# Attention, routed experts and a dense layer in one kernel: early routing moved up, three quarter buffers, and dense rows transposed elsewhere

## The chip, the cores and the metric

One core of a Trainium2 chip. Its engines are PE (matrix multiply), DVE (vector), ACT (activation), POOL (GpSimd) and SP, which here issues most of the DMA. The metric is the device time of one execution in microseconds (us), as a median of runs.

## What is computed

```python
q, k, v: (4, 12, 448, 64) float32
attn = sigmoid(q @ k.T / 8 - log(448)) @ v          # per batch and head
x = attn.transpose(0, 2, 1, 3).reshape(1792, 768)   # tokens
logits = x @ w_gate                                 # 8 experts
e = argmax(logits); g = softmax(logits)[e]          # top 1
x[t] = g[t] * relu(x[t] @ w1[e[t]]) @ w2[e[t]]      # w1 768x1024, w2 1024x768
out = relu(x @ w_in) ** 2 @ w_out                   # 768x2048, 2048x768
```

## The kernel before

All matmuls of the experts and of the dense layer are made three times on a high and a low half of each operand: `split_w` (L461) lets ACT copy the float32 chunk into the high half (L462) and DVE, or POOL where asked, subtract it for the low half (L463). The instructions of each engine run in the order in which the program writes them (a manual schedule), so an engine that waits holds back all that is written behind it. SP's DMA issues are such a queue too.

**Attention** runs over 24 units, one for each batch and pair of heads (loop from L477, n = 0 to 23, `last_n` = 23). In unit n, PE computes the scores of n in four parts, ACT the sigmoids, and PE the products with v of unit n-1 (`av_step`). `rows` (L408) transposes the result of unit n-2 and sends it to x_d in DRAM through ACT (L413, two buffers). After the last pair of a batch `logits` (L383) adds up the gate logits into the tile lgT, of which there is one buffer, and `token_logits` (L400) turns them into one row per token. Beside this, `convert` rewrites the dense weights chunk by chunk: nine of 16 (PRE = 9) in units 2 to 19, the last of them on DVE to the end of unit 19. The other seven follow in steps taken by `rest` (L597).

**Early routing.** After batch 2, `head` (L186) finds each token's expert from the first 12 of 16 groups of rows and adds up the counts (`cum`), `counts` (L200) sums them on PE into p1, which uses lgT's buffer, `early_expert` (L219) picks the fullest expert, `spots` (L211) and `pick_rows` (L215) find its first 256 tokens, and `early_rest` (L234) copies the result from p1. Slots 0 and 1 work on these tokens, so their weights can be loaded (`regs`, `reload`, L304 to L311) and their rows gathered (`early_gather`) while attention still runs. The full routing of all tokens (`head`, `counts`, `slots` L244, `late_places` L260, `spots`, `pick_rows`, `late_rows`) takes place during slot 0 in the function `opening` (L855), and its rest (`late_routing` L790, `quarters` L815, `gates` L827) during slot 2.

**Slots.** NBASE = 15 slots of 128 tokens of one expert each (loop from L884). A slot has eight steps: `up(0)` to `up(3)` multiply by w1, `down(4)` to `down(7)` by w2, each with one weight chunk of 128 x 1536. Between them `htrans` (L679) transposes the hidden rows on PE, ACT writes the high half hh (L683) and DVE the low half hl (L684), for each half of the hidden layer (hl 0 and hl 1 in the prediction). After each step `next_chunk` splits the next slot's chunk, which lies in `raw[c]`, and reloads `raw[c]` for the slot after that, if its expert differs. Chunk 7 is split on POOL (`POOL_W`). At step 5 `xtrans` (L291) transposes the next slot's rows through the two px tiles. In slot 0, `take` splits chunks 4 to 7. From slot 3 on, four *quarters* of 32 leftover tokens are worked off between the steps (`q_event` L743): each has its own eight weight chunks, read from QB = 2 buffers `qraw` by `q_load` (L732), and each load is issued when the buffer before it has been used.

**Into the dense layer.** The slots write their result to y_d. In the last slot (s = 14) the weight ring for the dense layer is filled (`stage`, `load_next`), `rest` takes eight steps, and `trans_y` (L605) transposes the first four row tiles of y_d: one behind the up half, three behind steps 4 to 6. Its two halves lie in weight tiles wh2, wh3, wl2, wl3 (`alloc_y`, L615). Then comes a block `If` (L934) for slots beyond 15, not taken here, and the quarters' writes to y_d on POOL (L954), one after the other. In the dense stage, block 0 has 1024 rows in two halves h: `layer1` (L995) runs 16 times, with four places for `rest` in each (two chunks of conversion take 16). The second half of t_d may be loaded only when all 16 chunks are done (L564).

## Time and profile before

| | us |
|---|---|
| median of 3 runs | 1017.72 |
| lowest, highest | 1012.18, 1018.63 |
| the profiled execution | 1016.02 |
| its span, first to last instruction | 1014.5 |
| PE busy in it | 954.3 |

The profile is of one execution. Its times count from the start of the span. Attention ends on PE at 172.47, slot 0 starts at 185.49, slot 1 at 215.49, slot 2 at 233.92, slot 3 at 261.13, the last slot at 514.93, and the dense stage at 549.95. In the rows, `<-` behind an operation names what was read, and `[4.65 <-POOL Bg L811]` is idle time ahead of it and what ended it. PEld is the loading of PE's weights, and a `q` behind an engine's name its instruction queue. The clock is given as a share of 2.4 GHz.

### The profile page before, as it was taken

Reading aid. Unit: us, or ns where it says so; the run is one execution under the profiler, and the core shown is the slowest. Engines: PE = TensorE matmul, PEld = TensorE weight load, DVE = VectorE, ACT = ScalarE, POOL = GpSimd, SP = SyncE. Lnnn points to the kernel's source line nnn. Section 1 sums busy time; section 2 is a strip of 40 time slices with the busy share of each in tenths; the row PEclk is TensorE's granted clock in tenths of the full one; section 3 lists DMA queues with packets and bytes.
Section 4 is the critical chain, followed back from the end, with each engine's and each line's share of the span. In section 5 each row is a group of like instructions: output and inputs, shape, how many; then the busy total and the mean of one; then the engine's idle time right before and its main releaser. Section 6 shows DMA issues by size and latency. Waiting matters only on the chain.

```text
span 1014.5 us, 15007 instructions
## 1 busy us (share of the span) xinstructions
PE 954.3 (94%) x5869; PEld 799.5 (79%) x5869; DVE 632.4 (62%) x692; ACT 551.2 (54%) x667; POOL 132.1 (13%) x120
## 2 busy tenths in 40 slices
PE   7999999788999999989987799999999999999996
PEld 3555554677887887878876688889999999999996
DVE  3777776668776666775766367626776632227863
ACT  5676665545776676775743354435544434446540
POOL 1000000214422222222220000000000110000002
PEclk9999999888999999998997899999999999999998
DMA  8788868271377769694457446442333442222412
GB/s 291 264 303 326 317 205 287 110 279 51 130 264 273 287 246 338 212 357 145 142 221 271 169 155 230 175 187 68 94 104 130 173 165 68 67 67 94 125 32 93
DMA packets 52512, 190.62 MB, mean 188 GB/s; under 512 B 8083, under 2 KB 18963, under 8 KB 50387
## 3 DMA queue, kind: packets, MB, share of 16 engines
q1 hardware_dynamic: 34290, 152.77, 43.1%
q0 software_dynamic: 6928, 31.08, 8.0%
q10 hardware_dynamic: 11216, 5.75, 2.0%
q8 instruction: 48, 0.79, 0.3%
q14 instruction: 30, 0.24, 0.1%
HBM read 203.33 MB, written 36.98 MB: 237 GB/s over the span
## 4 chain that ended last, share of the span: by engine, by line
PE 75%; DMA 10%; issue 8%; DVE 3%; ACT 2%; POOL 1%; SPq 0%; POOLq 0%; another core or an unknown queue 0%; ACTq 0%; DVEq 0%
PE pq L1103 7%; PE pq L1104 7%; PE pq L1105 7%; PE pp L1003 6%; PE pp L1004 6%; PE pp L1005 6%; PE po L373 5%; PE sc L363 5%; DMA qraw<-in_wm 4%; PE ph L654 3%; PE py L654 3%; PE py L656 3%; PE ph L655 3%; PE py L655 3%; PE ph L656 3%
## 5 line engine op out<-in xcount | busy, mean ns | idle before, releaser
L463 DVE TENSOR_TENSOR wl<-raw,wh 128x1536 fp32r<-128x1536 f32 x98 | 193.1, 1974 | 83.9 <-ACT wh L462 74.6
L462 ACT ACTIVATE wh<-raw 128x1536 fp32r<-128x1536 f32 x112 | 165.9, 1482 | 4.2 <-PE ph L656 2.0
L367 ACT ACTIVATE a<-sc,bias_s 128x896 f32<-128x896 f32 x96 | 82.5, 910 | 55.3 <-PE sc L363 55.1
L1009 ACT ACTIVATE r<-pp 128x512 f32<-128x512 f32 (+1 forms) x64 | 34.8, 544 | 117.0 <-PE pp L1005 117.0
L654 PE MATMUL py<-wh,hh 128*128 128x384 f32 x240 | 88.2, 368 | 3.9 <-ACT hh L683 3.9
L1103 PE MATMUL pq<-wrh,sh 128*128 128x384 f32 x264 | 89.0, 337 | 0.3 <-DVE raw L1064 0.3
L1104 PE MATMUL pq<-wrl,sh 128*128 128x384 f32 x264 | 88.6, 336 | 0.0
L1105 PE MATMUL pq<-wrh,sl 128*128 128x384 f32 x264 | 88.6, 336 | 0.0
L656 PE MATMUL py<-wh,hl 128*128 128x384 f32 x240 | 84.1, 350 | 3.9 <-DVE hl L684 3.9
L655 PE MATMUL py<-wl,hh 128*128 128x384 f32 x240 | 83.7, 349 | 1.3 <-DVE wl L463 1.3
L654 PE MATMUL ph<-wh,xh 128*128 128x512 f32 x180 | 76.9, 427 | 0.0
L463 DVE TENSOR_TENSOR wrl<-raw,wrh 128x1536 fp32r<-128x1536 f32 x30 | 52.7, 1757 | 36.0 <-ACT wrh L462 36.0
L655 PE MATMUL ph<-wl,xh 128*128 128x512 f32 x180 | 72.7, 404 | 0.0
L656 PE MATMUL ph<-wh,xl 128*128 128x512 f32 x180 | 72.7, 404 | 0.0
L462 ACT ACTIVATE wrh<-raw 128x1536 fp32r<-128x1536 f32 x30 | 44.5, 1483 | 47.8 <-PE pq L1105 43.1
L463 POOL TENSOR_TENSOR wl<-raw,wh 128x1536 fp32r<-128x1536 f32 x14 | 49.0, 3500 | 164.6 <-ACT wh L462 164.6
L1030 DVE TENSOR_TENSOR sl<-h,sh 128x1024 fp32r<-128x1024 f32 (+1 forms) x56 | 59.8, 1086 | 8.7 <-ACT sh L1029 8.6
L1017 DVE TENSOR_TENSOR h<-h,h 128x512 f32<-128x512 f32 (+1 forms) x16 | 10.0, 625 | 88.5 <-ACT h L1012 88.5
L373 PE MATMUL po<-a,qkv 128*64 128x448 f32 x288 | 59.4, 548 | 0.0
L1029 ACT ACTIVATE sh<-h 128x1024 fp32r<-128x1024 f32 (+1 forms) x56 | 51.5, 943 | 13.6 <-PE pq L1104 8.0
L978 POOL DMA_INDIRECT out<-raw,idx x14 | 13.7, 978 | 330.8 <-DVE raw L1064 302.3
L1003 PE MATMUL pp<-why,wrh 128*128 128x512 f32 (+1 forms) x132 | 49.2, 373 | 7.5 <-issue 7.5
(274 smaller groups left out, 2200.9 us busy)
## 6 DMA issues: line engine op xcount, KB each, us to landing
raw<-in_wm SPq DMA_DIRECT2D x112, 768.0 KB
qraw<-in_wm SPq DMA_DIRECT2D x32, 768.0 KB
raw<-t_d SPq DMA_DIRECT2D x28, 768.0 KB
cs<-in_w SPq DMA_DIRECT2D x9, 1536.0 KB
raw<-w_d SPq DMA_DIRECT2D x16, 768.0 KB
qkv<-in_qk SPq DMA_DIRECT2D x23, 480.0 KB
raw<-in_w SPq DMA_DIRECT2D x7, 1536.0 KB
t_d<-raw POOLq DMA_DIRECT2D x7, 1536.0 KB, 7.6
```

The costliest lines, as they stand in the source:

```text
L367: nc.scalar.activation(a[:, :n], ps[:, :n, :S], AF.Sigmoid, bias=bias_s, scale=1.0 / math.sqrt(D))
L373: nc.tensor.matmul(po[64 * h:64 * h + 64, :S], vr[:, 128 * c + 64 * h:128 * c + 64 * h + 64], a[:, h], start=(c == 0), stop=False, skip_gr ...
L462: nc.scalar.activation(h, src, AF.Copy)
L463: (nc.gpsimd if pool else nc.vector).tensor_tensor(l, src, f32(h), op=ALU.subtract)
L654: nc.tensor.matmul(ps, lh, rh, start=first, stop=False)
L655: nc.tensor.matmul(ps, lh, rl, start=False, stop=False)
L656: nc.tensor.matmul(ps, ll, rh, start=False, stop=last)
L1003: nc.tensor.matmul(pp[:, :N], lh, rh, start=(k == 0), stop=False)
L1004: nc.tensor.matmul(pp[:, :N], lh, rl, start=False, stop=False)
L1103: nc.tensor.matmul(po[p][:, :DH], lh, wc[:, w0:w0 + DH], start=(q == 0 and kk == 0 and o in (0, 2, 5)), stop=False, **fl)
L1104: nc.tensor.matmul(po[p][:, :DH], lh, wcl[:, w0:w0 + DH], start=False, stop=False, **fl)
L1105: nc.tensor.matmul(po[p][:, :DH], ll, wc[:, w0:w0 + DH], start=False, stop=(q == 3 and kk == 1), **fl)
```

## The change

There are five parts. (1) Early routing: `token_logits` and `head` run at the end of unit 19, `counts`, `early_expert` and `spots` in unit 20, `pick_rows` in unit 21, `early_rest` and both early gathers at the start of unit 22; each of them was a unit later (the gathers stood behind the last unit in the program, though POOL issued them at once). Chunks 0 and 1 of the early expert are loaded in unit 21 into a tile `first` that later is a weight tile, the others go into raw[0] to raw[5]; chunks 0 to 2 are split at the ends of units 21 to 23. (2) Behind the last unit slot 0's rows are transposed between its products, ahead of both row copies; then come the full `head` and the split of chunk 3. (3) In `opening`, counts and slots move to step 0, POOL no longer splits a chunk, spots stays at step 5, and `pick_rows`, `late_rows` and two gathers move to slot 1; `late_routing` moves from slot 2, step 0, to slot 1, step 6, `quarters` to slot 2, step 0, and `gates` with the first quarter loads to step 5. (4) QB is 3; the tile Bg lies in one of the three buffers until gates has read it. (5) In the last slot the four `trans_y` stand behind steps 0 to 3, their two halves lie in the raw buffers of chunks 4 to 7, no `rest` runs there, conversion uses two weight tiles instead of raw buffers, and the loads of the next two row tiles are issued at step 4.

```diff
@@ -43,7 +43,7 @@
-QB = 2
+QB = 3
@@ -162,7 +162,7 @@
-    gp, Bg = rt([CP, NR, 3], "gp", BF16), rt([CP, NR, 3, LC], "Bg", BF16)
+    gp = rt([CP, NR, 3], "gp", BF16)
@@ -303,14 +303,24 @@
-        if s:
+        if s > FS:
...
+    def chunk0(c):
+        return raw[c - 2] if c > 1 else first[:, c * CH:(c + 1) * CH]
...
     def reload(s, c):
-        more_ = dict(cond=regd[s], cond_hint=False) if s else {}
-        nc.sync.dma_start(out=raw[c], in_=wm[ds(rege[s], 1), :, c].rearrange("a p n -> (a p) n"), **more_)
...
+        more_ = dict(cond=regd[s], cond_hint=False) if s > FS else {}
+        dst = raw[c] if s else chunk0(c)
+        nc.sync.dma_start(out=dst, in_=wm[ds(rege[s], 1), :, c].rearrange("a p n -> (a p) n"), **more_)
...
+    def rtile(k, name, dt=F32):
+        return rawp.tile([128, 2 * CH], dt, tag=f"raw{k}", name=name)
...
+    def wpair(w, dt, name):
+        return w1p.tile([128, 2 * CH], dt, tag=f"{w}p", name=name)
@@ -462,6 +472,13 @@
+        def split_first(c):
+            split_w(chunk0(c), wh[c], wl[c])
+            if c == 1:
+                for w, l in (("wh", wh), ("wl", wl)):
+                    both = wpair(w, F32R, f"{w}23")
+                    l.extend([both[:, :CH], both[:, CH:]])
@@ -472,20 +489,25 @@
             if n >= len(units) - 4:
-                rawb.append(rawp.tile([128, 2 * CH], F32, tag="raw", name=f"raw{n}", bufs=4))
+                rawb.append(rtile(n % 4, f"raw{n}"))
...
-                wh, wl = ([w1p.tile([128, CH], F32R, tag=f"{w}{c}", name=f"{w}{c}") for c in range(4)] for w in ("wh", "wl"))
+                wh, wl = ([w1p.tile([128, CH], F32R, tag=f"{w}{c}", name=f"{w}{c}") for c in range(2)] for w in ("wh", "wl"))
+                first = wpair("wl", F32, "first")
+            if n == last_n - 2:
+                regs(0)
+                reload(0, 0)
+                reload(0, 1)
             if n == last_n - 1:
-                regs(0)
-                for c in range(4):
-                    reload(0, c)
+                reload(0, 2)
+                reload(0, 3)
+                early_rest(pr1)
+                xg = {s: early_gather(s) for s in range(FS)}
...
-                early_rest(pr1)
@@ -493,10 +515,7 @@
-            if n == last_n:
-                logits(b, GJ - 1)
-                split_w(raw[0], wh[0], wl[0])
-            elif done and n < last_n - 1:
+            if done:
@@ -504,43 +523,43 @@
-            if due:
+            if due or n == last_n - 4:
                 token_logits()
-            if n == last_n - 2:
+            if n == last_n - 3:
...
+            if n == last_n - 2:
+                pick_rows(pr1, Bt1, FR)
...
+            if n == last_n - 4:
+                head(0, FR)
             if n == last_n - 3:
-                head(0, FR)
-            if n == last_n - 2:
...
-            if n == last_n - 1:
-                pick_rows(pr1, Bt1, FR)
-            if n == last_n:
-                split_w(raw[1], wh[1], wl[1])
+            if n > last_n - 3:
+                split_first(n - last_n + 2)
...
-        extras()
-        for c in range(4):
-            av_step(c)
+        av_step(0)
+        av_step(1)
+        xs = {}
+        tx = [ps_s.tile([128, 2, 512], F32, tag="sc", name=f"tx{i}")[:, 0].rearrange("p (b c) -> p b c", b=4) for i in range(2)]
+        xs[0] = xtrans(0, xg.pop(0), tx)
+        av_step(2)
+        av_step(3)
...
         reload(0, 7)
+        extras()
...
-        xg = {s: early_gather(s) for s in range(FS)}
-        xs = {}
-        tx = ps_s.tile([128, 2, 512], F32, tag="sc", name="tx").rearrange("p a (b c) -> p a b c", b=4)
-        xs[0] = xtrans(0, xg.pop(0), [tx[:, 0], tx[:, 1]])
         token_logits()
-        split_w(raw[2], wh[2], wl[2])
+        head(FR, NR)
+        split_first(3)
...
-        head(FR, NR)
-        split_w(raw[3], wh[3], wl[3])
@@ -580,9 +600,9 @@
         if step < 7:
-            narrow(n, step, rawb[2], rawb[3], None)
+            narrow(n, step, *cv, None)
         if step == 4 and n < 15:
-            narrow(n + 1, 0, rawb[2], None, None)
+            narrow(n + 1, 0, cv[0], None, None)
@@ -596,8 +616,8 @@
         if pool is None:
-            n = 3
-            t = [[wtile(f"{w}{c}", f"{w}y_{bi}_{c}") for c in (2, 3)] for w in ("wh", "wl")]
+            n = 6
+            t = [[x] for x in ([rtile(k, f"yt{k}", F32R) for k in (2, 3)] if bi == 0 else [wpair(w, F32R, f"{w}y_{bi}") for w in ("wh", "wl")])]
@@ -608,17 +628,18 @@
-        per = 3 if n == 3 else 4
+        per = 3 if n == 6 else 4
...
-            for j in js[::n]:
-                dst = yh[j // n][:, :, t * 128:(t + 1) * 128]
-                src = pt[:, j - js[0]:j - js[0] + n]
+            w = min(n, per)
+            for j in js[::w]:
+                dst, low = (x[j // n][:, j % n:j % n + w, t * 128:(t + 1) * 128] for x in (yh, yl))
+                src = pt[:, j - js[0]:j - js[0] + w]
...
-                nc.vector.tensor_tensor(yl[j // n][:, :, t * 128:(t + 1) * 128], src, f32(dst), op=ALU.subtract)
+                nc.vector.tensor_tensor(low, src, f32(dst), op=ALU.subtract)
@@ -807,6 +826,8 @@
+            Bg = mp.tile([128, 2 * CH], BF16, tag="qraw", name="Bg", bufs=QB)[:CP, :NR * 3 * LC].rearrange("p (t a s) -> p t a s", t=NR, a=3)
+            qt["Bg"] = Bg
@@ -824,9 +845,9 @@
         def gates():
-            pg = ps_x.tile([128, 4, 128], F32, tag="px1", name="pgt").rearrange("p a b -> p (a b)")
+            pg = ps_q.tile([128, 512], F32, tag="q", name="pgt")
             for t in range(NR):
-                nc.tensor.matmul(pg[:, :3 * LC], A[:, t, :], Bg[:, t].rearrange("p a s -> p (a s)"), start=(t == 0), stop=(t == NR - 1))
+                nc.tensor.matmul(pg[:, :3 * LC], A[:, t, :], qt["Bg"][:, t].rearrange("p a s -> p (a s)"), start=(t == 0), stop=(t == NR - 1))
@@ -842,32 +863,29 @@
-        def take(c, pool=False):
-            split_w(raw[c], mh[c], ml[c], pool=pool)
+        def take(c):
+            split_w(chunk0(c), mh[c], ml[c])
...
             if c == 0:
-                early_gates()
-                take(4)
-            elif c == 1:
...
-            elif c == 2:
-                take(5)
...
-                take(7, pool=True)
-            elif c == 3:
-                take(6)
-                late_places(prk2)
-                for k in range(8):
-                    reload(FS, k)
+                reload(FS, 0)
+                reload(FS, 1)
+                reload(FS, 6)
+                reload(FS, 7)
+                take(4)
+                early_gates()
+            elif c < 4:
+                take(4 + c)
+                if c == 3:
+                    for k in range(2, 6):
+                        reload(FS, k)
+                    late_places(prk2)
...
-            elif c == 7:
-                pick_rows(pr2, Bt, NR)
-                late_rows(pr2)
-                xg[FS] = gather(FS)
@@ -875,38 +893,38 @@
-            if 0 < s and s + 2 < NBASE:
-                if s > 1:
-                    regs(s + 2)
+            if 1 < s and s + 2 < NBASE:
+                regs(s + 2)
...
+            if last:
+                ynext = alloc_y(0)
...
+                if s == 1 and c == 0:
+                    pick_rows(pr2, Bt, NR)
+                    late_rows(pr2)
+                    for k in range(FS, FS + 2):
+                        xg[k] = gather(k)
...
                     if c == 0:
-                        late_routing()
-                    elif c == 1:
...
                     elif c == 3:
-                        gates()
-                        nc.gpsimd.dma_start(out=yq_d[:, :, DM:DM + 1].rearrange("q t a -> t q a"), in_=tok[:QM, NSLOT:].bitcast(F32).unsqueeze(2))
-                        for n in range(QB):
-                            q_load(n)
...
                 if last:
-                    rest()
+                    trans_y(0, 0, c, ycur[0][c], ynext, ps_x, ("px0", "px1"))
             if last:
-                ynext = alloc_y(0)
-                trans_y(0, 0, 0, ycur[0][0], ynext, ps_x, ("px0", "px1"))
+                cv.extend(wpair(w, F32, f"{w}c") for w in ("wh", "wl"))
+                narrow(PRE, 0, cv[0], None, None)
@@ -914,21 +932,25 @@
+                if s == FS and c == 5:
+                    gates()
+                    nc.gpsimd.dma_start(out=yq_d[:, :, DM:DM + 1].rearrange("q t a -> t q a"), in_=tok[:QM, NSLOT:].bitcast(F32).unsqueeze(2))
+                    for n in range(QB):
+                        q_load(n)
...
+                if s == 1 and c == 6:
+                    late_routing()
...
-                if last and c < 7:
-                    trans_y(0, 0, c - 3, ycur[0][c - 3], ynext, (ps_x, ps_h)[c % 2 == 0], ("px0", "px1") if c % 2 else ("ph0", "ph1"))
+                if last:
+                    if c == 4:
+                        yns = {t: load_y(0, 1, t, xgp, 2, "xg") for t in range(2)}
...
-                if last:
-                    rest()
-            if last:
-                yns = {t: load_y(0, 1, t, xgp, 2, "xg") for t in range(2)}
@@ -1049,7 +1071,9 @@
-        obs = [[rawb[2 + h][:, p * DM:(p + 1) * DM] for p in range(P)] for h in range(2)]
+        if bi == 0:
+            ob = [rtile(k, f"ob{k}") for k in (2, 3)]
+        obs = [[ob[h][:, p * DM:(p + 1) * DM] for p in range(P)] for h in range(2)]
```

## Rows read from the trace of the kernel before

**Rows 1.** The page, part 1: busy us of each engine, share of the span, instructions.
```profile
PE 954.3 (94%) x5869; PEld 799.5 (79%) x5869; DVE 632.4 (62%) x692; ACT 551.2 (54%) x667; POOL 132.1 (13%) x120
```

**Rows 2.** Waits of PE over the span: who, for whom, us in total, times, longest.
```profile
PE pp L1003 <- issue: 7.5, 1, 7.5
...
PE qa L761 <- DMA qraw<-in_wm: 7.5, 3, 3.6
...
PE pyt L616 <- DMA yn<-y_d: 6.9, 1, 6.9
...
PE pgt L829 <- POOL Bg L811: 4.7, 1, 4.7
...
PE py L654 <- ACT hh L683: 3.9, 1, 3.9
```

**Rows 3.** Windows: stretch, length, busy PE, PEld, DVE, ACT, POOL, clock, DMA share, GB/s.
```profile
172.47:185.49 13.02, 8.51 (x42) 4.46 (x43) 4.75 (x6) 4.47 (x7) 0.00 (x0) 0.90 0.94 344
185.49:215.49 30.00, 23.86 (x119) 20.55 (x119) 23.79 (x60) 13.08 (x17) 7.06 (x6) 0.82 0.29 106
215.49:233.92 18.43, 18.43 (x104) 16.71 (x101) 12.86 (x12) 13.86 (x15) 3.66 (x3) 1.00 0.61 236
233.92:261.13 27.21, 22.28 (x116) 19.72 (x116) 22.18 (x40) 15.63 (x18) 13.66 (x12) 0.87 0.26 91
261.13:514.93 253.80, 242.68 (x2008) 207.28 (x2007) 177.97 (x121) 175.35 (x193) 69.39 (x35) 0.97 0.68 245
514.93:542.40 27.47, 23.56 (x117) 20.91 (x116) 16.97 (x21) 12.47 (x19) 5.28 (x2) 0.88 0.52 177
549.95:585.50 35.55, 28.69 (x117) 23.57 (x117) 16.71 (x27) 10.51 (x22) 3.00 (x5) 0.83 0.52 178
```

**Rows 4.** The same view, three stretches right behind a long wait of PE.
```profile
457.60:462.80 5.20, 5.19 (x33) 3.98 (x34) 0.00 (x0) 0.00 (x0) 1.17 (x2) 0.50 0.90 318
528.48:534.47 5.99, 5.99 (x21) 5.67 (x22) 5.26 (x7) 1.96 (x5) 0.00 (x0) 0.50 0.17 33
577.00:582.30 5.30, 5.29 (x19) 4.72 (x20) 2.90 (x9) 1.98 (x6) 0.00 (x0) 0.50 0.00 2
```

**Rows 5.** DVE in order of time, units 19 to 22: start, us, line, operation.
```profile
147.61 0.56 DVE L130 TENSOR_TENSOR cd<-cd 128x384 f32<-128x384 f32 x1
...
151.67 0.24 DVE L191 TENSOR_REDUCE m<-lg 112x12 f32<-112x96 f32 x1
...
153.65 0.44 DVE L197 TENSOR_TENSOR_SCAN cum<-seg,ohz 112x136 bf16<-112x136 bf16 x1
...
161.21 2.08 DVE L213 TENSOR_SCALAR A<-iot,plf 112x128 f16<-112x128 f16 x12
```

**Rows 6.** Chain that ended last, end of attention: start, us, what.
```profile
149.15 0.70 PE lgT L405 x8
...
172.56 8.63 DMA x_d<-xn
```

**Rows 7.** Slot 0, in order of time: POOL, then DVE.
```profile
199.94 3.49 POOL L463 TENSOR_TENSOR wl<-raw,wh 128x1536 fp32r<-128x1536 f32 x1 [3.63 <-ACT wh L462]
...
200.01 3.46 DVE L257 CAST ctl<-esl 128x20 int32<-128x20 f32 x1
```

**Rows 8.** Quarter loads: SP in order of time, then the chain that ended last.
```profile
292.03 0.34 SPq L739 DMA_DIRECT2D qraw<-in_wm  x1
...
300.25 8.97 DMA qraw<-in_wm
```

**Rows 9.** POOL in order of time: the last slot, then two t_d writes.
```profile
517.16 3.50 POOL L463 TENSOR_TENSOR wl<-raw,wh 128x1536 fp32r<-128x1536 f32 x1 [13.82 <-ACT wh L462]
...
592.18 0.90 POOL L131 DMA_DIRECT2D t_d<-raw  x1 [23.20 <-DVE raw L130]
...
663.25 0.89 POOL L131 DMA_DIRECT2D t_d<-raw  x1 [15.59 <-DVE raw L130]
```

**Rows 10.** Line 934 (the If): duration min/median/max in ns, first and last start.
```profile
L934 PEldq COMPARE_BRANCH  x1: 5262/5262/5262, 539.5 to 539.5; - x1
```

More of the change, by code (lines that the diff above doesn't have):

```diff
@@ L334, in load @@
         def load(b, j):
-            rv = rawp.tile([128, 2 * CH], F32, tag="raw", name=f"qkv_{b}_{j}", bufs=4)
+            rv = rtile((b * NP + j) % 4, f"qkv_{b}_{j}")
             r = rv[:, :QW]
```

3 lines of the change are left out of this document (1 added, 2 removed).

## Prediction

> **What bounds the kernel now.** I read the page first, then PE's waits, then windows cut at the borders of the stages, and only then single engines. The page says that PE is busy 954.3 of 1014.5 us [rows 1]: nothing else can be the bound on the whole, and the change can win only the 60 us in which PE stands, plus what it loses at half clock. The list of waits names where [rows 2]: 7.5 us at the first dense matmul, 7.5 us in the first layer of the quarters (weights not landed), 6.9 us for rows of y_d, 4.7 us for the gate products, 3.9 us in the last slot behind ACT. The windows show the same by stage [rows 3]. Slot 1 is the clean one: 18.43 us, PE never idle, clock 1.00; that is the price of a slot without quarters. Slot 0 takes 30.00, slot 2 27.21, the last slot 27.47, and 13.02 lie between the last unit's end and slot 0. After a long wait PE runs on at a granted clock of 0.50, the 1.2 GHz level [rows 4]; there each us yields half. So a wait costs itself and some 2.5 to 3 us behind it.
>
> **The change part by part.** The sum is made against the profiled execution, 1016.02 us (span 1014.5 and 1.5 around it), which lies 1.7 below the median 1017.72. A plus is time lost.
>
> *Early routing a unit sooner (units 19 to 22), +3.9.* PE is never idle here, so each new wait is a loss. DVE ends the w_out conversion at 148.17 (147.61 + 0.56), and head takes 2.42 (151.67 to 154.09) [rows 5]. Now token_logits comes a unit earlier (0.70 on PE [rows 6], moved, not added), and head runs straight behind the conversion: cum is ready at 148.2 + 0.7 + 2.4 = 151.3. PE asks for it with counts where its scores end, 149.15 + 0.70 = 149.85 [rows 6]: 1.4 of wait. Behind head, and a unit on behind spots (2.08 of DVE [rows 5]), the split of the next q and k comes late by about 0.5 in all (estimate from the same durations). Third, logits now opens a new lgT tile in unit 22, which frees only when early_rest has copied pr1; on DVE early_rest stands behind the first weight split, which waits for ACT, which waits for the last sigmoid and for chunk 0. I follow the queues to 2.0 of wait. If chunk 0 needed the 9.0 from issue to landing that a weight load needs under load [rows 8] and not the some 4 that I assume, it would be 7. Bounds of this part: +1 and +8. Queued behind the waiting split on ACT are the sigmoids, for which PE waits in turn. SP has no other work there (all q, k, v loads are out), POOL's two gathers move up with nothing behind them.
>
> *Between the last unit and slot 0, -5.1.* PE is busy 8.51 of 13.02, part of it at the low clock [rows 3]. In the chain the 8.63 us of an x_d write end the wait [rows 6]: ACT stands before the row copy, and the transposed x of slot 0 stands behind it. Now that x is transposed before both row copies, its gather is out somewhat earlier, and chunks 0 to 2 are split. I count 6.3 of PE work and 1.6 of waits (logits on the last xT, DVE being behind split 2): 7.9. Bounds -7 and -2.
>
> *Slot 0, -7.2.* DVE is busy 23.79 of 30.00 [rows 3]. One CAST of 20 columns took 3.46 us because POOL's split of chunk 7 (3.49) ran beside it [rows 7]; one of the twelve small operations of spots takes 0.17 [rows 5]. The change gives that split to DVE and drops chunk 2's, so DVE keeps about 20.5 us, more than PE's 18.43. The queue order (slots and two splits ahead of hl 0, late_places ahead of hl 1) adds some 2.3: 22.8. Bounds 18.9 (PE alone) and 27. Slot 2's eight weight loads lose their condition; they ran before too (slots 0 and 1 moved 30.00 us at 106 GB/s and 18.43 at 236 [rows 3], 7.5 MB, of which 6.3 are such weights). The Trainium skill's page "SBUF — State Buffer", section "SBUF: two separate sides", says that GpSimd and VectorE share one port pair, that whoever starts first holds it for the whole instruction, and that the other stands still. By that rule the 3.46 goes wholly, as the row says, but it comes back in slot 2, below.
>
> *Slots 1 and 2, +0.4 and -2.3.* pick_rows (some 0.4) moves into slot 1. late_routing moves from slot 2 to the end of slot 1, quarters to slot 2's start, gates to its second half. The wait for the gate products (4.7 [rows 2]) goes, but what is late next is hl 0: ahead of it DVE has the same work, late_routing, two splits and quarters, in all 22.18 busy in 27.21 [rows 3]; only the idle time of DVE at slot 1's end (18.43 against 12.86 busy) is won. I take a wait of 3.5 and 1.5 of low clock on 18.43 + 0.5 (gates) + 1.0 (order on PE): 24.9. Bounds: 22 and 27.4. If POOL's products and its split of chunk 7 each stop DVE wholly, as the quoted rule has it, 3.5 comes on top and the part wins nothing.
>
> *Three quarter buffers, -15.0.* Slots 3 to 13: 253.80, PE busy 242.68, so 11.1 idle, nearly all of it for quarter weights, and a clock of 0.97, up to 7.6 lost, of which I count 5 (one such stretch is 5.20 at 0.50 [rows 4]). The worst kind of load was issued at 300.25 and landed 8.97 later, too late by a wait of the order of 2 to 3.6 [rows 2, 8]. With three buffers each load is issued at the place of the one before, here 292.03 [rows 8], 8 us sooner: more than any wait. The number of loads is the same. Bounds -16.5 and 0.
>
> *Last slot, -5.5.* Without the conversion steps ACT no longer stands before the copy of hh: 3.9 of wait and half of 5.99 [rows 2, 4] go, 6.9. The four tiles' transposes are the same number of instructions, now in the up half. Their low parts go where chunk 7 lies, which POOL reads until 520.66 [rows 9], 5.7 us into the slot; DVE waits, the second tile's transposes wait for their px tile: 1.4 back. Bounds -7 and -3.
>
> *Into the dense stage, -1.0 and -8.5.* PE stands 7.5 at line 934. Its branch alone took 5.26 [rows 10], and the DMA rings were full with a 1.5 MB t_d write, which now comes later; I take 1.0 (0 to 4). The Trainium skill's "Runtime: NRT & Kernel Launch", section "Instruction fetch mechanics", says that a taken branch has to wait for its code by DMA; by it the gap stays and the sum is 1.0 less. The wait for rows of y_d (6.9, then half of 5.30 [rows 2, 4]) goes: POOL no longer stands at the If for the t_d write, its four quarter writes start some 9 sooner, and two of the loads are issued in the last slot. I take 8.5 of 9.5; bounds 0 and 9.5.
>
> *Rest of the dense stage, +0.7.* Eight conversion steps move here, 56 into 64 places. Their DVE time is hidden behind PE. The last t_d write comes two calls later: its cover is gone by some 16 us, see below. 0 to +4.
>
> Sum: +3.9 - 5.1 - 7.2 + 0.4 - 2.3 - 15.0 - 5.5 - 1.0 - 8.5 + 0.7 = -39.6. 1016.0 - 39.6 = 976.4 for a profiled execution, 978 with the 1.7 of the median.
>
> **The rivals.**
> 1. *Quarter loads stay late.* When a slot's weights are reloaded too, the DMA engines run at a share of 0.90 and more (first row of [rows 4]); an earlier issue would only queue longer. For it: the low stretches lie there. Against: the mean share of slots 3 to 13 is 0.68 [rows 3]. Time: 978 + 15 = 993.
> 2. *The early part gives it back.* Chunk 0 lands late and ACT stands before the sigmoids (+4.1), slot 0 is 27 (+4.2), POOL stops DVE in slot 2 (+2.3): 978 + 10.6, about 989. For it: DVE is the fuller engine in slots 0 and 2. Against: the splits 0 to 2 are out of the way. The Trainium skill's page "SBUF — State Buffer" stands on its side for the third term.
> 3. *The dense rows are late all the same*, as the quarters' writes to y_d still end last: the 9.5 stay, 978 + 9.5, about 988.
> 4. *Slower: conversion ends last.* All seven chunks are now converted inside dense layer 1 of block 0, and the loads of the second half of t_d wait for the last write. A chunk is eight steps, two calls of sixteen; the last is done in call 14, and write and load leave some 5 us of margin. Four cycles took 71.07 together, 17.8 each [rows 9], where 17.1 would be the pace. It decides from 17.1 + (39.6 + 5) / 7 = 23.5 a cycle; at 26 it costs 7 x 8.9 - 5 = 57, which gives 1035. Against: a cycle would have to grow by half.
>
> **How the numbers follow.** Forecast 0.55, its own range 968 to 987. Rival 1 0.13, rival 2 0.15, rival 3 0.06, rival 4 0.05; several of the first three with other losses, ending within 1% of before, 0.06. About 1% (10 us) is what a measurement of this kernel can tell from no change. Faster by more: 0.55 + 0.13 + 0.15 + 0.06 = 0.89; within: 0.06; slower: 0.05. The range of 8 in 10 takes the forecast and rivals 1 to 3 without their worst ends, and on the low side parts with better bounds (-4 in slot 0, -3 at the If, -2 between): 964 to 999.
>
> **What would show it.** Right: waits on qraw gone and slots 3 to 13 near 237 to 239; slot 0 near 23; last slot near 22, with a wait of DVE on POOL's split in its first third; no wait on yn; no CAST over 1 us in slot 0; new waits of PE on cum in unit 20 and on the copies of pr1 in unit 22. Wrong: PE standing on hl in slot 2 as long as before, loads of qraw landing over 12 us after issue, a wait of the first pq on the split of ring chunk 9, or attention longer by over 8 us.

## The result, and the profile after

The changed kernel takes 982.77 us (median of four, 979.62 to 985.92) against 1017.5 for the kernel before (four runs, 1012.18 to 1018.63): a ratio of 0.967, 95% interval 0.962 to 0.972. The forecast was 978, its range 964 to 999. The profiled execution took 985.92 us with a span of 984.1, which is 30.4 less than before, where 39.6 had been worked out.

First the waits of PE over the whole span of the changed kernel (who, for whom, us in total, times, longest).

```profile
PE py L677 <- DVE hl L703: 8.4, 4, 6.0
PE sc L373 <- DMA qkv<-in_qk: 5.9, 1, 5.9
PE pyt L636 <- DMA yn<-y_d: 5.8, 1, 5.8
PE lgT L401 <- DVE sa L237: 4.9, 1, 4.9
PE pp L1027 <- issue: 4.4, 1, 4.4
PE p L201 <- DVE cum L197: 1.4, 1, 1.4
PE pyt L636 <- DVE yt L642: 1.3, 1, 1.3
```

Against [rows 2]: the waits on qraw, on Bg and on hh are gone. The 5.9 at sc is the first load of the kernel, which no part of the change touches. New are sa (the copies of pr1, in unit 22), cum and yt. The waits on yn and at the branch are smaller, but they stayed. The wait on hl has moved and grown: 6.0 of it now lie in slot 2, where the kernel before had its longest, 3.3, in slot 0 (at 209.01) and 0.3 in slot 2:

```profile
PE py L656 <- DVE hl L684: 3.9, 3, 3.3
```

Next the windows, cut at the stages as in [rows 3] (length, busy us of PE, PEld, DVE, ACT, POOL, granted clock, DMA share, GB/s): end of attention to slot 0, slots 0, 1 and 2, slots 3 to 13, the last slot; then three stretches at half clock, each of which begins while PE still waits (until 166.43, 244.77 and 546.69); then the dense stage from PE's return after the branch.

```profile
180.98:188.76 7.78, 7.65 (x43) 3.59 (x43) 4.47 (x6) 3.69 (x6) 0.00 (x0) 1.00 0.82 265
188.76:210.58 21.82, 19.43 (x103) 16.54 (x103) 20.34 (x60) 12.36 (x15) 3.56 (x5) 1.00 0.62 234
210.58:229.48 18.90, 18.90 (x115) 16.98 (x115) 12.87 (x12) 14.08 (x16) 3.71 (x3) 1.00 0.39 140
229.48:256.39 26.91, 20.95 (x115) 18.83 (x115) 23.61 (x40) 15.63 (x18) 12.60 (x11) 0.87 0.16 50
256.39:493.91 237.52, 237.15 (x2008) 203.19 (x2007) 177.94 (x121) 175.34 (x193) 68.10 (x37) 1.00 0.73 267
493.91:516.07 22.16, 20.81 (x117) 18.15 (x116) 10.91 (x17) 11.24 (x18) 3.61 (x2) 1.00 0.46 165
...
163.33:170.15 6.82, 3.72 (x12) 0.96 (x14) 4.21 (x9) 2.91 (x3) 2.72 (x2) 0.50 0.86 329
241.83:248.66 6.83, 3.89 (x13) 3.79 (x14) 6.15 (x7) 0.00 (x0) 2.73 (x2) 0.51 0.25 72
...
545.62:552.45 6.83, 5.76 (x20) 4.94 (x21) 3.44 (x10) 1.98 (x6) 0.00 (x0) 0.50 0.12 48
521.83:984.10 462.27, 447.50 (x2386) 421.66 (x2386) 257.29 (x280) 205.86 (x273) 22.06 (x25) 0.98 0.37 130
```

In the kernel before, the gap at the branch and the dense stage:

```profile
542.40:549.95 7.55, 0.00 (x1) 0.29 (x1) 3.43 (x6) 2.06 (x2) 0.96 (x1) 0.65 0.91 325
549.95:1014.50 464.55, 448.64 (x2388) 422.28 (x2387) 250.91 (x273) 203.96 (x272) 21.13 (x24) 0.98 0.36 124
```

Slots 3 to 13 are the prize: PE idles 0.37 us in 237.52, at full clock, where it idled 11.1 in 253.80. Slot 2 stands out: as long as before, with 6 us of idle PE, DVE busy 23.61 of 26.91, and 6.83 us at a clock of 0.51, of which 3.9 lie behind the wait.

Each term of the forecast against the two profiled executions (the span changed by -30.4, their sum):

| term | forecast | measured | read from |
|---|---|---|---|
| units 19 to 22 | +3.9 | +8.5 | attention ends at 180.98, was 172.47 |
| to slot 0 | -5.1 | -5.2 | 7.78, was 13.02 |
| slot 0 | -7.2 | -8.2 | 21.82, was 30.00 |
| slot 1 | +0.4 | +0.5 | 18.90, was 18.43 |
| slot 2 | -2.3 | -0.3 | 26.91, was 27.21 |
| slots 3 to 13 | -15.0 | -16.3 | 237.52, was 253.80 |
| last slot | -5.5 | -5.3 | 22.16, was 27.47 |
| the If's gap | -1.0 | -1.8 | 516.07 to 521.83, was 542.40 to 549.95 |
| rows of y_d, rest of the dense stage | -7.8 | -2.3 | 462.27, was 464.55 |

Three terms missed by 2 us or more: units 19 to 22, slot 2, and the rows of y_d. The experiments go to these three, to the largest term, and to the branch. The terms from attention's end to slot 1 and of the last slot were not undone alone: they rest on these windows and waits.

### The profile page after: what moved, and what is told of

The parts are those of the page before. It is cut to its first block, busy times and chain, and to the rows that moved or that the text cites. A ratio compares the mean times of both kernels' runs of the same rounds, so it can differ in the third digit from the quotient of the medians.

```text
span 984.1 us, 15011 instructions
## 1 busy us (share of the span) xinstructions
PE 941.8 (96%) x5869; PEld 786.9 (80%) x5869; DVE 632.2 (64%) x693; ACT 552.1 (56%) x667; POOL 125.3 (13%) x119
## 5 line engine op out<-in xcount | busy, mean ns | idle before, releaser
L473 DVE TENSOR_TENSOR wl<-raw,wh 128x1536 fp32r<-128x1536 f32 x97 | 189.4, 1957 | 62.5 <-ACT wh L472 59.8
L472 ACT ACTIVATE wh<-raw 128x1536 fp32r<-128x1536 f32 x110 | 163.2, 1483 | 4.1 <-PE ph L677 1.5
L677 PE MATMUL py<-wh,hl 128*128 128x384 f32 x240 | 82.1, 342 | 8.4 <-DVE hl L703 8.4
L675 PE MATMUL py<-wh,hh 128*128 128x384 f32 x240 | 85.1, 355 | 0.0
L676 PE MATMUL py<-wl,hh 128*128 128x384 f32 x240 | 81.3, 339 | 0.0
L675 PE MATMUL ph<-wh,xh 128*128 128x512 f32 x180 | 74.9, 416 | 0.0
L473 POOL TENSOR_TENSOR wl<-raw,wh 128x1536 fp32r<-128x1536 f32 x13 | 45.5, 3499 | 130.9 <-ACT wh L472 117.1
L1000 POOL DMA_INDIRECT out<-ob,idx x14 | 13.7, 979 | 315.1 <-DVE ob L1088 286.4
L677 PEld LDWEIGHTS py<-wh,hl 128*128 128x128 f32 x240 | 45.5, 190 | 9.7 <-DVE hl L703 9.7
```

What stands on the lines that cost most here:

```text
L472: nc.scalar.activation(h, src, AF.Copy)
L473: (nc.gpsimd if pool else nc.vector).tensor_tensor(l, src, f32(h), op=ALU.subtract)
L675: nc.tensor.matmul(ps, lh, rh, start=first, stop=False)
L676: nc.tensor.matmul(ps, lh, rl, start=False, stop=False)
L677: nc.tensor.matmul(ps, ll, rh, start=False, stop=last)
```

## The experiments

### The same kernel again, and with two quarter buffers

> The changed kernel once more, unaltered, as the yardstick for the three runs beside it: 980 to 986 us, with a wait of PE of some 4.9 us on the copies of pr1 near 166, some 6 us on hl in slot 2 and some 5.8 us on yn. If these three waits differ by over 1 us from the first profile, readings of 1 us in the other runs mean nothing.

Measured: 981.84 us (979.03 to 985.43). The waits in unit 22 (4.4) and on hl (6.0) are back. The wait on yn is not: in this execution PE doesn't wait for it at all, and the dense stage takes 454.61 us from PE's return after the branch, 7.7 less than in the first profile. So this one wait comes and goes between executions of one kernel; the section on the rows of y_d below looks at what goes with it.

```profile
522.59:977.20 454.61, 445.62 (x2386) 420.14 (x2386) 257.57 (x280) 205.90 (x273) 22.11 (x25) 0.99 0.37 132
```

The eight times of this kernel so far lie in two groups of four, 979.03 to 980.75 and 984.02 to 985.92. A median that differs from this kernel's by 3 to 4 us is therefore not clear of its spread, and in what follows the windows and waits are read first. Slots 0 to 13 differ by at most 0.4 each between the two profiles.

```diff
-QB = 3
+QB = 2
```

> Two quarter buffers in place of three, all else as changed. My theory, the forecast's own term: the third buffer is what removed the waits on quarter weights, worth about 15 us in slots 3 to 13: they go from 237.5 back to 250 to 254, PE waits some 7 us on qraw, and the time is 996 to 1000. Rival: the loads come in time for another reason (the first ones are now issued in slot 2's down half, and slot 2's own eight loads are out earlier), and the buffer is worth little: slots 3 to 13 within 3 us of 237.5, time 983 to 986.

Measured: 994.41 us (991.25 to 998.45), 12.6 above the repeat on the same chip. The windows over slots 3 to 13 (same columns), and two of PE's waits:

```profile
258.00:512.31 254.31, 241.70 (x2007) 206.50 (x2007) 177.92 (x121) 175.52 (x193) 71.11 (x37) 0.98 0.69 249
```
```profile
PE qa L780 <- DMA qraw<-in_wm: 8.9, 4, 3.3
...
PE qb L800 <- DMA qraw<-in_wm: 3.3, 2, 2.5
```

254.31 is 16.8 more than the 237.51 of the repeat, and the 253.80 of before to within 0.5. The median rose by less, and lies under the 996 expected; the spans of the two profiled executions differ by 19.8, and runs of either kernel by 6 to 7. The buffer alone is this term; the earlier first loads and slot 2's unconditional loads give nothing here. Rival 1 of the forecast (loads only queue longer) is out: with three buffers the DMA share of these slots rose to 0.73, and PE waited for none of them.

### Unit 22: who holds the logits

The timeline of the changed kernel around the wait (start, us, engine, line; in brackets the idle time before and its releaser):

```profile
157.34 0.90 SPq L315 DMA_DIRECT2D first<-in_wm  x2
...
162.96 1.48 ACT L472 ACTIVATE wh<-first 128x1536 fp32r<-128x1536 f32 x1 [3.17 <-DMA first<-in_wm]
...
164.48 1.76 DVE L473 TENSOR_TENSOR wl<-first,wh 128x1536 fp32r<-128x1536 f32 x1 [3.71 <-ACT wh L472]
166.15 0.15 DVE L235 CAST idx<-p 128x4 uint32<-128x4 f32 x1
```

The chain is read from below: the three copies that free pr1 take 0.15 each, but stand on DVE behind a split, the split behind ACT, ACT behind chunk 0, which landed at 162.96, 5.6 after its issue at 157.34.

```diff
                 reload(0, 2)
                 reload(0, 3)
-                early_rest(pr1)
-                xg = {s: early_gather(s) for s in range(FS)}
...
+            if n == last_n - 2:
+                early_rest(pr1)
+                xg = {s: early_gather(s) for s in range(FS)}
             if n > last_n - 3:
                 split_first(n - last_n + 2)
```

> The copies of pr1 (early_rest) and the two early gathers go ahead of the split of chunk 0, at the end of unit 21. My theory: PE's wait of 4.9 us at the logits of unit 22 is there only because these copies stand on DVE behind a split that waits for chunk 0 (ACT idle 3.2, then 1.5 and 1.8 us of split). Then the wait goes, and with it most of the 3.4 us lost in the 6.8 us at half clock behind it; ACT still stands for chunk 0 with the sigmoids behind it, which I price at 2: slot 0 starts 5 to 7 us sooner, time 975 to 978. Rival: chunk 0 itself holds PE, by way of ACT and the sigmoids; PE's wait only moves to the scores or the products of unit 22, slot 0 starts at most 2 us sooner, time 981 to 983.

Measured: 978.61 us (975.91 to 981.27), 3.2 below the repeat on the same chip. The wait on sa is gone, slot 0 starts at 183.47, 5.3 before the first profile and 6.0 before the repeat, and the clock is 1.00 from 159.05 on. In this run too, ACT stands for chunk 0, and DVE's split behind it (163.71), but the copies are done by then:

```profile
160.49 0.15 DVE L235 CAST idx<-p 128x4 uint32<-128x4 f32 x1
...
162.19 1.48 ACT L472 ACTIVATE wh<-first 128x1536 fp32r<-128x1536 f32 x1 [2.61 <-DMA first<-in_wm]
```

ACT still idles 2.61 for the chunk, but PE waits for sigmoids only 0.3 us in this kernel. The late chunk cost PE through one place alone: three small copies queued behind its split. The median fell by less than the 5 to 6 us. The profiled execution has a wait of PE on yn again (5.1 in two); against the first profile, which has it too, its span is 4.7 shorter (979.4 against 984.1).

### Slot 2: the shared port or the length of DVE's queue

The timeline of the changed kernel in slot 2, POOL, DVE, then PE:

```profile
235.30 2.28 POOL L832 TENSOR_TENSOR Bg<-Bs,gp 112x384 bf16<-112x384 f16 x1 [0.62 <-DVE gp L828]
237.53 3.45 POOL L473 TENSOR_TENSOR wl<-raw,wh 128x1536 fp32r<-128x1536 f32 x1
...
236.79 4.25 DVE L838 TENSOR_TENSOR cmq<-srow,qs 128x32 f32<-128x32 f32 x1
...
244.77 0.69 PE L677 MATMUL py<-wh,hl 128*128 128x384 f32 x1 [5.96 <-DVE hl L703]
```

An operation on 32 columns takes 4.25 us and ends 0.06 after POOL's split (237.53 + 3.45 = 240.98). Three kernels take the two causes apart. The first:

```diff
-        def split_m(c):
-            split_w(raw[c], mh[c], ml[c], pool=(c in POOL_W))
+        def split_m(c, pool=True):
+            split_w(raw[c], mh[c], ml[c], pool=pool and c in POOL_W)
...
-                split_m(c)
+                split_m(c, s > 1)
```

> In slot 1 chunk 7 of the next weights is split by DVE, not by POOL. My theory: DVE's first operation of the quarters took 4.25 us at 236.79, where its like takes under 0.2, because POOL's product (2.28) and split (3.45) ran beside it and kept it from its memory port; without POOL's split it ends with the product, at about 237.6, so 3.4 us are saved and 1.8 for the split are added: hl is ready 1.6 us sooner, the wait of 6.0 becomes 4.0 to 4.6, slot 2 is 24.5 to 25.5, time 980 to 981.5. Rival: the 4.25 is that operation's own, or something else's on DVE; then it stays over 3, the added split makes hl later by 1.8, the wait is 7 to 8 and the time 983 to 985.

Measured: 978.26 us (977.13 to 982.69). DVE in slot 2:

```profile
234.82 4.08 DVE L473 TENSOR_TENSOR wl<-raw,wh 128x1536 fp32r<-128x1536 f32 x2
238.82 0.18 DVE L838 TENSOR_TENSOR cmq<-srow,qs 128x32 f32<-128x32 f32 x1
```

The same operation takes 0.18. The wait fell to 4.2, as expected, but slot 2 only to 26.22 (24.5 to 25.5 expected): the stretch at low clock behind the wait did not shrink with it (PE busy 21.98 for the same work, 20.95 in the changed kernel). The median is 3.6 below the repeat's, which was taken on another chip. Slot 2's 0.7 to 1.1 can't explain that, so it says nothing on slot 2.

```diff
                 if s == FS:
-                    if c == 0:
+                    if c == 2:
                         quarters()
                         q_gather(0)
```

> quarters and the first quarter gather stand behind hl 0 of slot 2 (third up chunk instead of first); POOL keeps its split. Theory of the shared port: the stall falls on the next large DVE operation instead, the split of chunk 1 at 238, which then ends near 242.7, hl at 243.4: the wait is still 4.5 to 5.5, slot 2 25.5 to 26.5, time within 1.5 of the unaltered kernel. Rival, the length of DVE's queue alone: with 5.8 us of quarters gone from ahead of it hl is ready at 238.5 to 240, the wait is under 1.5, slot 2 is 20 to 21.5, time 975 to 977.

Measured: 982.35 us (978.54 to 985.13), slot 2 at 24.91, the wait 4.4, hl at 243.38. POOL, then DVE:

```profile
238.39 3.45 POOL L473 TENSOR_TENSOR wl<-raw,wh 128x1536 fp32r<-128x1536 f32 x1
...
235.97 7.48 DVE L473 TENSOR_TENSOR wl<-raw,wh 128x1536 fp32r<-128x1536 f32 x2
```

Now it is two splits that take 7.48, where two take 3.42 to 3.52 elsewhere, and hl follows at 243.38. The theory of the port had put it at 243.4, but in a slot that started 0.9 earlier; the wait and the slot are a little below its 4.5 to 5.5 and 25.5 to 26.5. With DVE's queue alone the wait would have been under 1.5. That POOL's split holds DVE back is shown; the queue adds to it, as the third kernel shows, which takes the work out of slot 2:

```diff
                 if s == 1 and c == 0:
+                    late_routing()
+                    quarters()
                     pick_rows(pr2, Bt, NR)
...
-                        quarters()
                         q_gather(0)
...
-                if s == 1 and c == 6:
-                    late_routing()
```

> late_routing and quarters both stand at the start of slot 1, ahead of the copies of its picked rows, where DVE stood idle for 3.2 us; slot 2 keeps only its splits and the gate products. Theory: slot 2's wait is DVE work in the wrong place; about 5.4 us of it fit into slot 1's idle 6 us. Slot 2 becomes 19 to 20.5 with a wait under 1, slot 1 19 to 20, time 974 to 977. Rival: the wait moves into slot 1 (hl 0 of slot 1 behind the longer queue, or the gather for slot 2 behind the copies, so that slot 2 starts late): slots 1 and 2 together lose less than 3 of their 45.8 us, time 979 to 982.

Measured: 978.47 us (977.52 to 984.88). Slot 2 takes 19.56 with a wait on hl of 0.4, but slot 1 takes 24.20, together 2.0 less than the 45.8. POOL and PE at its end:

```profile
218.66 5.46 POOL L832 TENSOR_TENSOR Bg<-Bs,gp 112x384 bf16<-112x384 f16 x3
224.28 2.36 POOL L664 DMA_INDIRECT xg<-x_d,idx  x1 [0.15 <-issue]
...
229.61 1.12 PE L297 MATMUL px<-ident,xg 128*128 128x128 f32 x6 [3.29 <-DMA xg<-x_d,idx]
```

Each theory held in one slot. The rival's wait is there, by a queue that neither had named: the three products moved along on POOL, ahead of the gather for slot 2's rows, which now went out at 224.28 instead of 218.57.

### The rows of y_d: which of two transfers goes first

In the chain of work that ended last, the changed kernel has these links at the dense stage's start:

```profile
516.81 7.12 DMA y_d<-y
...
534.27 4.46 DMA y_d<-yq_d
...
539.18 7.38 DMA yn<-y_d
```

The row write of the last slot, four quarter writes that each wait for the one before (the last one issued at 534.27), and the load. Just ahead of the load stands POOL's 1.5 MB t_d write of chunk 9, issued at 538.53. Over the executions so far, and those of the runs on slot 2, the wait goes with the order of these two:

| execution | t_d write | yn loads | PE's wait on yn |
|---|---|---|---|
| first profile | 538.53 | 539.18 | 5.8 |
| copies of pr1 early | 533.70 | 533.96 | 5.1 |
| quarters behind hl 0 | 537.00 | 538.63 | 6.0 |
| two buffers | 557.16 | 556.86 | 1.9 |
| the repeat | 539.61 | 538.29 | 0 |
| POOL's split to DVE | 538.23 | 536.96 | 0 |
| late_routing early | 539.64 | 538.21 | 0 |

Loads that go out 1.3 us or more ahead of the write are in time; those that follow it land some 7 us after their issue; 0.3 ahead is in between. In the kernel before, a t_d write (there chunk 10's) was ahead too, with a wait of 6.9. POOL, then SP:

```profile
555.61 0.56 POOL L954 DMA_DIRECT2D y_d<-yq_d  x1 [11.24 <-DVE raw L114]
...
568.06 0.92 POOL L131 DMA_DIRECT2D t_d<-raw  x1
...
570.09 1.62 SPq L593 DMA_DIRECT2D yn<-y_d  x2
```

A third transfer lies in the same stretch, SP's 1.5 MB load for the next conversion chunk:

```profile
531.95 0.33 SPq L101 DMA_DIRECT2D whc<-in_w  x1
```

The last quarter write, issued 2.3 behind it, took the 4.46 to land, with the DMA engines at a share of 1.02 from 534 to 536 us. Last write to yn loads took 4.9 here and 5.3 in the repeat, but 2.3 to 2.4 in the two kernels below that send this load out behind the yn loads (the second one of this section, and the first attempt on the last version). Both of them move the t_d write back as well, so no run has the one without the other: that the order of the t_d write alone makes the wait is argued from the table, not shown. Two kernels try to use it:

```diff
-            if bi == 0 and c < 2 and h == 0:
-                for t in (2 * c, 2 * c + 1):
+            if bi == 0 and c in (0, 2) and h == 0:
+                for t in (c, c + 1):
```

> The transposes of the dense rows' tiles 2 and 3 of the second half stand one layer-1 call later (8.5 us); the loads and writes of y_d stay where they are. My theory: the chain of y_d writes (row write of the last slot 7.1 us, four quarter writes 14.7, load 7.4) is as long as before and only its cover was short: the wait of 5.8 us and the 2.9 lost in some 5.8 us at half clock go, 7 to 9 us in all, time 974 to 977. Rival: the loads move along (a buffer that is freed by the first tiles' transposes, or SP held by another load), PE waits at the later place, gain under 2 us, time 981 to 983.

Measured: 985.81 us (985.09 to 986.83). No wait on yn, but in this execution the loads went out 1.9 ahead of the write, so there may have been none to take away; and no gain, the four runs lie with the slower group of the unaltered kernel. The first call that reads these tiles now stands right behind their transposes, and PE waits 2.6 for ACT's copy of them, followed by a stretch at a lower clock (0.66 from 555.5 to 565). Neither theory had that; the call between the transposes and their use had been cover too.

```diff
-    todo = [(n, k) for n in range(PRE, 16) for k in range(1, 9)]
+    todo = [(n, k) for n in range(PRE, 16) for k in ((7, 8, 1, 2, 3, 4, 5, 6) if n == PRE else range(1, 9))]
```

> The steps that convert chunk 9 in the dense stage stand two steps (about 4 us) later: its two empty steps come first instead of last; the number of steps is the same. My theory: PE waits for yn only in runs where the 1.5 MB t_d write of chunk 9 is issued ahead of the yn loads (first profile: write at 538.53, loads at 539.18, landed 7.4 us later; the unaltered repeat: loads at 538.29, write at 539.61, no wait; the run with the copies ahead: write at 533.70, loads at 533.96, wait 5.1). With the write 4 us later the loads are first every time: no wait on yn, all runs at the fast end, median 977 to 980 and the runs within 3 us. Rival: the loads land some 7 us after their issue whatever lies ahead of them, because the chain of y_d writes sets it; the wait stays in some runs, median 981 to 984.

Measured: 985.92 us (983.11 to 988.35). No wait on yn, as expected, yet no gain: its runs lie around the slower group of the unaltered kernel. DVE, then PE, of this run:

```profile
552.64 0.96 DVE L112 TENSOR_SCALAR wlc<-whc 128x1536 uint32<-128x1536 uint32 x1 [6.77 <-DMA t_d<-wlc]
...
557.62 0.50 PE L1025 MATMUL pp<-hy,wrh 128*128 128x512 f32 x1 [3.40 <-ACT r L1031]
```

The two empty steps behind a chunk are the time in which its write leaves the one buffer. Without them DVE stands for the write, ACT behind DVE with a conversion operation, and the relu, for which PE waits, behind that.

### The branch

Left out: the optional slots under the If (seven; the expectation miscounts), which this input doesn't take, and the branch.

```diff
-        with tc.If(more < NT):
-            for s in range(NBASE, NSLOT):
...
```

> The six optional slots under the If are left out, the branch with them; the quarter writes stay. My theory: the gap at the first dense matmuls (0.7 and 4.1 to 5.1 us of PE in the runs so far) is the branch and the code behind it; without it PE goes from the last slot into layer 1 with under 1 us lost, and the 3.4 us at half clock behind it (1.7 lost) go too: the dense stage starts 5 to 6 us sooner, time 976 to 978. But the quarter writes and the yn loads hang on the last slot's row write, not on PE: with 5 us less cover PE waits for yn in every run, 5 us and more, which gives most of it back; then 980 to 983 with a gap under 1 us. Rival: PE waits there for something else than the branch (the first split in the ring, the transposed rows): the gap stays over 3 us, time 981 to 984.

Measured: 982.0 us (981.58 to 983.36). The gap at the first dense matmuls is gone from the list of waits, and one row has grown:

```profile
PE pyt L636 <- DMA yn<-y_d: 8.4, 1, 8.4
```

The gap is the branch's, and taking it away won nothing here: PE arrives some 5 us earlier at rows whose loads went out behind the t_d write in this execution (536.73 against 534.88). The Trainium skill's page "Runtime: NRT & Kernel Launch", section "Instruction fetch mechanics", says that a taken branch has to wait for its code by DMA where its target is not among the code already fetched. This run agrees in so far as the gap goes with the branch; that it is code that PE waits for, no run shows.

### A version from these parts

The copies of pr1 ahead of the split, and late_routing and quarters at slot 1's start, both as above; and POOL's three products in a function of their own, behind the two gathers:

```diff
+        def gate_parts():
             Bg = mp.tile([128, 2 * CH], BF16, tag="qraw", name="Bg", bufs=QB)[:CP, :NR * 3 * LC].rearrange("p (t a s) -> p t a s", t=NR, a=3)
...
                     for k in range(FS, FS + 2):
                         xg[k] = gather(k)
+                    gate_parts()
```

> The copies of pr1 ahead of the first split, and late_routing and quarters at slot 1's start with POOL's three gate products behind the two gathers, so that the wait of 3.3 us for x rows in the run with late_routing early is gone. Theory: slot 0 starts 5 to 6 us sooner, as measured alone; slots 1 and 2 together take 39 to 40 us in place of 45.8 to 46.2; the dense stage as before, with the wait for yn in some runs. Time 969 to 972. Rival: POOL's products, now at 222 to 228, keep DVE from its splits in slot 1's down half and make hl 1 or the x of slot 2 late, so slots 1 and 2 stay over 42 us and the time over 973.

Measured: 972.65 us (969.16 to 974.18), a ratio to the kernel before of 0.958, interval 0.955 to 0.962, and 9 to 10 us below the changed kernel; its slowest run is 4.9 below the fastest of that kernel. Slots 0, 1 and 2:

```profile
183.22:205.11 21.89, 19.38 (x102) 16.54 (x102) 20.70 (x61) 12.36 (x15) 3.38 (x4) 1.00 0.64 238
205.11:225.58 20.47, 19.04 (x115) 16.81 (x115) 18.43 (x36) 14.16 (x16) 6.42 (x6) 1.00 0.34 124
225.58:245.18 19.60, 19.22 (x116) 17.15 (x115) 16.54 (x15) 15.60 (x17) 11.26 (x8) 1.00 0.22 70
```

Slots 1 and 2 take 40.07 instead of 45.8, all at full clock, and slot 0 starts 5.5 sooner. The write of chunk 9 went out at 527.21, the yn loads at 527.27, and PE waits 3.6. Two attempts at this wait, each on top of this version:

```diff
-    todo = [(n, k) for n in range(PRE, 16) for k in range(1, 9)]
+    todo = [(PRE, 7), (PRE, 8)] + [(n, k) for n in range(PRE, 16) for k in range(1, 9)]
```

> As the run beside it, and two empty conversion steps ahead of chunk 9's in the dense stage, with the two empty ones behind each chunk kept (58 steps of 64 places). Theory: the t_d write of chunk 9 is issued some 4 us behind the yn loads in every run, so PE never waits for yn; and unlike the run that took the empty steps from behind the chunk, the write has its time to land before chunk 10 is begun, so no wait on the relu. Time 966 to 969, all runs within 4 us. Rival: the conversion as a whole is 4 us later and ACT or the last t_d loads hold PE: a wait of PE on r or on the ring of over 2 us, time 970 to 974.

Measured: 978.81 us (976.42 to 980.13). The wait on yn is gone, but PE waits 5.6 us in four places for the relu (longest 2.5), down to the end of layer 1: the rival, larger than it was put.

```diff
                     if c < 6:
                         stage(c - 4)
-                        load_next()
+                    if c == 7:
+                        load_next()
```

> As the run with both routing moves (copies of pr1 early, late_routing and quarters in slot 1), and in the last slot the loads of two ring chunks (1.5 MB, issued some 3 us ahead of the row write) stand behind the row write. Theory: the row write landed 6.6 to 7.3 us after its issue because those loads fill the DMA engines (share 0.87 to 1.09 from 504 to 508 us in that run); first on its queue it lands in 2.5 to 4, so the quarter writes and the yn loads come 3 to 4 us sooner, always ahead of the t_d write of chunk 9: no wait for yn (3.6 in that run's profile), time 966 to 970. Rival: something else holds the row write, or the moved loads now stand before the branch's code and lengthen the gap at the first dense matmuls by 2 us or more: 971 to 975.

Measured: 976.33 us (975.23 to 977.98). SP's load for the next conversion chunk and the quarter writes on POOL in this run:

```profile
519.96 0.33 SPq L101 DMA_DIRECT2D whc<-in_w  x1
...
515.38 0.56 POOL L980 DMA_DIRECT2D y_d<-yq_d  x1 [23.82 <-SPq L960]
520.91 0.53 POOL L980 DMA_DIRECT2D y_d<-yq_d  x1 [4.97 <-DMA y_d<-yq_d]
527.00 0.50 POOL L980 DMA_DIRECT2D y_d<-yq_d  x1 [5.56 <-DMA y_d<-yq_d]
```

Row write at 508.62, first quarter write 6.8 later, as late as before, but the profile puts that wait down to SP at the branch (L960 there), and SP was issuing the ring loads until 515.06: when the row write landed isn't seen. The next two links took 5.5 and 6.1, where 3.1 to 4.8 and 2.4 to 3.4 were usual: the first with the ring loads under way, the second with the 1.5 MB load of 519.96. The yn loads went out 1.7 behind the t_d write, and PE waited 10.1. The gap at the branch fell to 2.0 and won nothing, as without the branch. Of the four kernels that aimed at the wait on yn, three are without it in their profiles, and none is faster than the kernel that it was built on.

## Why the forecast held, and where it did not

**The sum, -39.6.** It came out at -30.4 in the first profile and at -37.3 in the repeat's (span 977.2), which differ mainly by the wait on yn.

**Three quarter buffers, -15.0.** Right in cause and size: -16.3, and undone alone +16.8. PE's idle time fell by 10.8 and its busy time by 5.5, where 5 had been counted for the low clock.

**To slot 0, slot 0, slot 1, last slot.** -5.2, -8.2, +0.5 and -5.3 for -5.1, -7.2, +0.4 and -5.5. Two waits named beforehand are there at their sizes: cum 1.39 (1.4), the second tile's px 1.35 (1.4). The first of these terms is right by luck: 6.3 of PE's work and 1.6 of waits had been counted between attention and slot 0, and PE was busy 7.65 and idle 0.13; the two errors cancel. In slot 0 no CAST took over 0.2.

**Units 19 to 22, +3.9.** The mechanism was right (early_rest behind the first split, behind ACT, behind chunk 0), one size was off: "2.0 of wait" at the logits was 4.9, and the half clock around it, which this term left out, cost half of 3.72. With the 1.4 at cum that makes 8.2 of the 8.5. The forecast named the price if chunk 0 came late (7) and did not take it; attention longer by over 8 was one of its own signs of being wrong. The chunk took 5.6 to land, not 9.0, but it was issued at 157.34, though its expert's number was written by 154.6. SP read that number into a register in between, which took 2.07 us the first time (from 154.7) and 0.27 as a rule (shortest, median, longest in ns):

```profile
L305 SPq TENSOR_LOAD <-ctl x14: 263/273/2069, 154.7 to 458.5; - x14
```

The experiment shows that a late chunk need not have cost PE anything.

**Slot 2, -2.3.** The step that failed is the choice to leave out the port ("3.5 comes on top and the part wins nothing"). The profile shows it: a wait of 6.0 for 3.5, and nothing won. The Trainium skill's page "SBUF — State Buffer", section "SBUF: two separate sides", says that whichever of VectorE and GpSimd starts first keeps the shared ports for its whole instruction, among others for a VectorE operation with two inputs in SBUF where the GpSimd one reads SBUF too. The rows agree in both directions: a DVE operation of 0.18 us became 4.25 beside POOL's product and split, and POOL's product of 0.84 became 2.28 beside a DVE split that had started first. But the port is only part of the miss: with POOL's split gone the wait was still 4.2 and the slot 26.22. The remainder is DVE's own work and the products ahead of it: moved out, the slot takes 19.6.

**The rows of y_d, -8.5.** Rival 3 in one profile of this kernel, the forecast in the other; the two groups of times suggest about half of the executions each. The step that failed is "its four quarter writes start some 9 sooner". They wait for the last slot's row write: from the end of that slot they start 8.6 later (524.64 against 516.07), where before they started 13.2 later (555.61 against 542.40), 4.6 sooner, and PE came sooner too. The chain from the first quarter write to the load is as long as it was, 14.5 in both, and a t_d write stood ahead of the load before as after. In the repeat, where the loads go first, the dense stage is 9.9 shorter than before (454.61 against 464.55), and the forecast's 7.8 was too little.

**The If's gap, -1.0.** It fell by 1.8. The 5.26 of the branch [rows 10] were not all gap: it ended at 544.8, 2.4 into the 7.55, and in the changed kernel at 516.4, ahead of the 4.4:

```profile
L956 PEldq COMPARE_BRANCH  x1: 3622/3622/3622, 512.8 to 512.8; - x1
```

The run without it shows that the term was priced at the wrong place: as long as the yn loads come late, a shorter gap is a longer wait.

Of **rival 2** (989) two of three losses are real, chunk 0's and the port's; slot 0's is not. **Rival 4** stayed out: the conversion took 18.3 a cycle (t_d writes from 538.53 to 648.49) where 23.5 would have decided. But it has little room: begun two steps later, it made PE wait for the relu in two kernels, 3.4 and 5.6, and the second of them lost 6 us.

## What to carry to other kernels

On an engine that works in order, put small operations that free a buffer ahead of a large one that waits for a transfer: three copies of 0.15 us held PE for 4.9. Give POOL no large operation beside DVE work that ends last, and when work is moved, follow every queue that it is moved on: the gain in slot 2 was lost in slot 1 until POOL's products stood behind the gathers. Where a wait appears in one execution and not in the next, compare the issue times of the transfers in both before pricing it.

## What the runs showed of the hardware that was not expected

A chain of small dependent writes has no fixed price. One quarter write of 96 KB led to the next after 2.4 us in quiet stretches, after 5.5 with ring loads of 768 KB under way and after 6.1 with a 1.5 MB load, so clearing one link of such a chain lengthened the others.

Whether 0.8 MB of rows were loaded 1.3 us ahead of a 1.5 MB write or 0.1 to 1.9 us behind it went with no wait or 3.6 to 10.1 us of wait for PE. The unaltered kernel showed both orders in two executions, which fits the two groups of its eight times; that they are this alone was not shown.

Twice an operation of DVE that waited for POOL was not let in between two of POOL's: the one issued at 236.79 waited through the end of a product (to 237.58) and the whole split behind it (from 237.53). POOL's spans are rough, but the kernel with the quarters later shows the same, where two splits took 7.48.
